# Crossbar transposes ahead of later stores, GpSimd's work in another order, and one visit split in two, in a linear-attention and MLP kernel

## The chip, the core and the metric

The kernel runs on one core of a Trainium2 chip. The metric is the device time of one execution in microseconds. The engines are called TensorE (PE in the profile; its weight loads are PEld), VectorE (DVE), ScalarE (ACT), GpSimd (POOL) and SyncE (SP). Each takes its instructions in the order in which the program wrote them; they meet through semaphores. GpSimd and SyncE also issue DMAs: GpSimd all loads (they cast from 32-bit to 16-bit floats on the way), SyncE the stores and the crossbar transposes (a DMA that turns a 16-bit tile of SBUF around).

## The reference

Four sequences (B = 4) of 768 positions, 8 heads of 64 go through an attention with exponential decay, worked out in blocks of 64 positions with a state per head; its output, as 3072 tokens of 512, goes through a two-layer MLP with an exact GELU.

```python
for b in range(nb):                      # blocks of 64 positions
    intra = np.einsum('bhic,bhjc->bhij', qb, kb) * Dmask[None]
    intra = np.einsum('bhij,bhjd->bhid', intra, vb)
    inter = np.einsum('bhid,bhde->bhie', qb * lam_pow[None], kv_state)
    out[:, :, sl] = intra + inter
    kb_dec = kb * rev_pow[None]
    kv_state = lam_block[None, :, None, None] * kv_state + np.einsum('bhsd,bhse->bhde', kb_dec, vb)
h = x @ w_in                             # 512 -> 2048
g = 0.5 * h * (1.0 + erf(h * inv_sqrt2))
return g @ w_out                         # 2048 -> 512
```

## The kernel before

**Tiling.** A chunk is 128 positions (two blocks) of one sequence; chunk n belongs to group n // 4 and sequence n % 4. There are six groups (0 to 5) of four chunks. A group of 512 tokens goes through the MLP while the attention of the next group is worked out in between: the order of the work is written out by hand (the scheduler is off).

**The MLP of a group** (`mlp`) is a list of blocks. Sixteen are `mm1`: four matmuls (512 columns, or 384 where the fourth chunk's tokens are left for later) into a bank "mh" (two of them), and a GELU on ScalarE. In group 0 the first two, in group 1 the first four have 384 columns, and a "late" block, at index 4 and 6, does the remaining 128 columns of them. Then come sixteen `mm2` blocks of four matmuls, four for each chunk's output rows; after the fourth ScalarE copies the bank to `o_sb` and SyncE stores it. `run_blocks(blocks, ahead)` runs the blocks, and before block i whatever stands in `ahead[i]`. So group 1 has blocks 0 to 32, with mm2 from 17 on, and stores after blocks 20, 24, 28 and 32.

**The attention of a chunk n.** The loads of k, q (`ask("k8 q8")`, 128 KB each) and of the V of a whole group (`V2`, four loads) are issued by GpSimd. k and q are turned into `kT`, `qT`: for chunks 0 to 7 by TensorE with copies by ScalarE (`both`), from chunk 8 on by two crossbar transposes on SyncE (`request`, lines 198 and 199). GpSimd makes `vd` (V times decay, `decay_v`, line 220) and half of `k2` (k by block, `by_block`, line 206, two copies); the other half is made by VectorE (line 211) or, for chunks 5 to 7, by ScalarE (line 209).

**A visit.** `visit(f, d)` is one run of small 64x64 matmuls on TensorE: for chunk d the scores (`sc`, from kT, qT) and the two state updates (`kv`, from k2, vd), and, between them, for chunk f, visited as d before, the outputs (`o`). Four banks "at" are taken in turn by kv, sc and o. VectorE then masks the scores (`mask`), makes t = kv + state, `mid` (its 16-bit copy; in group 1 by ScalarE), empties f's outputs into `xT` (`empty`), which the next group's MLP reads, and makes the new state from t2 = kv + t. I write a visit as (f,d), with - for none. With a merged visit there are 64 matmuls that scores and outputs share; alone there are 32.

**The order before.** In group 0's mm2 blocks (index 17 on, two chunks' blocks by turns) stand `both(4)` before block 24, then before blocks 29, 30, 31, 32 the rest of group 1: visit (-,4) before 29, (4,5) before 30, (5,6) before 31, (6,7) before 32; the V loads of group 2 stand after k2 of chunk 6. In group 1: visit (7,-) before block 1, (-,8) before 6, then (8,9), (9,10), (10,11), (11,12) before 13, 19, 25, 31. Each `request` stands at the point where its chunk's GpSimd work does (before blocks 2, 8, 14, 20), followed by the loads of the chunk after next. In group g >= 2, with n = 4(g+1), visits (n,n+1) and so on stand before blocks 7, 15, 23, 31, and a chunk's request, GpSimd work and the loads two chunks on before 0, 8, 16, 24.

So SyncE's queue holds, for instance: transposes of 12 (block 20), the four stores of group 1, transposes of 13, 14, 15, two stores of group 2, transposes of 16. SyncE takes them one by one, each when its data is there.

**Buffers.** k and q ten each, V of groups three, kT, qT and k2 four each, vd six, `o_sb` three.

Of the kernel before, what the change touches and what calls it, by code (L numbers as in the profile page):

```python
# [8 lines left out]
F32 = mybir.dt.float32  # L9
# [6 lines left out]
def kernel(  # L16
# [29 lines left out]
    work_pool = ctx.enter_context(tc.tile_pool(name="work", bufs=4))  # L46
    x_pool = ctx.enter_context(tc.tile_pool(name="x", bufs=2))
    g_pool = ctx.enter_context(tc.tile_pool(name="g", bufs=2))
    out_pool = ctx.enter_context(tc.tile_pool(name="outp", bufs=3))
    ps = ctx.enter_context(tc.tile_pool(name="ps", bufs=1, space=bass.MemoryType.PSUM))  # L50

    BANKS = dict(mh=2, mo=2, at=4)
# [4 lines left out]
    def half(i):  # L57
        return slice(i * 64, (i + 1) * 64)
# [12 lines left out]
                                         bufs=B if name == "v" else 10)  # L71
        nc.gpsimd.dma_start(t, dram[name][b, :, g * C:(g + 1) * C, :].rearrange("h si d -> si h d"))  # L72

    def load_blocks(g, name):

        t = raw["group", g, name] = qkv_pool.tile([128, 2, B * HP, D], BF16, tag=name + "g", name=name + "g_t", bufs=3)
        src = dram[name].rearrange("b (hp hi) s d -> hi s (b hp) d", hi=2)
        for u in range(2):
            for hi in range(2):
                s = g * C + u * L  # L80
                nc.gpsimd.dma_start(t[half(hi), u], src[hi, s:s + L])  # L81
# [23 lines left out]
    def ask(items):  # L105

        for item in items.split():
            name, at = item[0], item[1:]
            if name in "kqv":
                load(int(at), name)  # L110
            elif name == "V":
                load_blocks(int(at), "v")
            else:
                (load_w_in if name == "i" else load_w_out)(*(int(x) for x in at.split("-")))

    ask("k0 q0 k1 q1 v0 k2 q2 v1 k3 q3 v2 v3 i0-2 i2-5 i5-8 i8-12 i12-16 o0-4 o4-8 o8-12 o12-16 "
        "k4 q4 V1 k5 q5 k6 q6 k7 q7")

    idle = consts.tile([128, 512], BF16)
# [57 lines left out]
    def begin(n):  # L177
        c = live[n] = Chunk()
        c.n, c.g, c.b = n, n // B, n % B
        c.q, c.k = (raw.pop((n, name)) for name in "qk")  # L180
        c.v = of_group(n, "v") if c.g else raw.pop((n, "v"))
        c.kT = work_pool.tile([128, HP, C], BF16, tag="kT", name="kT")
        c.qT = work_pool.tile([128, HP, C], BF16, tag="qT", name="qT")
        return c

    def transposed(c, name, tag, eng):

        t_ps = bank([128, HP, C], BF16, tag, "t_ps")
        src, dst = (c.k, c.kT) if name == "k" else (c.q, c.qT)
        for hp in range(HP):  # L190
            nc.tensor.transpose(t_ps[:, hp, :], src[:, 2 * hp:2 * hp + 2, :], ident)
        if eng is nc.scalar:
            nc.scalar.copy(dst, t_ps)
        else:
            eng.tensor_copy(dst, t_ps)

    def dma_transposes(c):
        nc.sync.dma_start_transpose(out=c.kT, in_=c.k.rearrange("p h d -> p (h d)"))
        nc.sync.dma_start_transpose(out=c.qT, in_=c.q.rearrange("p h d -> p (h d)"))

    def by_block(c):

        c.k2 = work_pool.tile([128, 2, HP, D], BF16, tag="k2", name="k2")
        k_r = c.k.rearrange("p (hp hi) d -> p hp hi d", hi=2)
        for hi in range(2):
            (nc.vector if c.n == B else nc.gpsimd).tensor_copy(c.k2[half(hi), hi], k_r[half(hi), :, hi, :])  # L206
        for hi in range(2):
            if c.g == 1 and c.n > B:
                nc.scalar.copy(c.k2[half(hi), 1 - hi], k_r[half(1 - hi), :, hi, :])
            else:  # L210
                nc.vector.tensor_copy(c.k2[half(hi), 1 - hi], k_r[half(1 - hi), :, hi, :])  # L211

    vd = {}

    def of_group(n, name):
        return raw["group", n // B, name][:, :, n % B * HP:(n % B + 1) * HP, :]

    def decay_v(n):
        vd[n] = work_pool.tile([128, 2, HP, D], BF16, tag="vd", name="vd", bufs=6)
        nc.gpsimd.tensor_mul(vd[n], of_group(n, "v"), lam_vb)  # L220


    def scores(c):
# [12 lines left out]
        return [[(kv[half(hi), u, hp, :], c.k2[half(hi), u, hp, :], vd[c.n][half(hi), u, hp, :], True)  # L236
                 for hi in range(2)] for u in us for hp in range(HP)]

    def next_states(c, between=lambda: None):
        s0 = state[c.n]  # L240
        t1 = work_pool.tile([128, HP, D], F32, tag="t1", name="t1")
        c.mid = work_pool.tile([128, HP, D], BF16, tag="mid", name="mid")
        if c.g == NG - 1:
            nc.vector.tensor_add(c.mid, c.kv[:, 0], s0)
            return between()
        nc.vector.tensor_add(t1, c.kv[:, 0], s0)
        if c.g == 1:
            nc.scalar.copy(c.mid, t1)
        else:
            nc.vector.tensor_copy(c.mid, t1)  # L250
        between()
        t2 = work_pool.tile([128, HP, D], F32, tag="t2", name="t2")
        nc.vector.tensor_add(t2, c.kv[:, 1], t1)
        new = state[c.n + B] = work_pool.tile([128, HP, D], BF16, tag="state", name="state", bufs=7)
        nc.vector.tensor_mul(new, t2, lam_cb)  # L255

    def outputs(c):
        o = c.o = bank([128, HP, C], F32, "at", "o_ps")
# [16 lines left out]
    def empty(c):  # L275
        nc.vector.tensor_mul(xT[c.g][:, :, c.b * C:(c.b + 1) * C], c.o, lam_o)  # L276
# [6 lines left out]
                    for out_, lhsT, rhs, start in pairs[i]:  # L283
                        nc.tensor.matmul(out_, lhsT, rhs, start=start, stop=True, skip_group_check=True)  # L284

    def visit(f, d):
        f, d = (live[n] if n is not None else None for n in (f, d))
        lists = []
        if d:
            kv = states(d)  # L290
            lists.append(scores(d) + kv)
        if f:
            lists.append(outputs(f))
        issue(*lists)
        if d is None or f and f.n == 2 * B - 2:
            empty(f)
            f = None
        if d:
            mask(d)
            next_states(d, lambda: f and empty(f))  # L300


    def scores0(n):
# [36 lines left out]
    def mlp(g, n3):  # L340
# [4 lines left out]
        def mm1(kf, hi=T):  # L345
            def run():
                h_ps = bank([128, T], F32, "mh", "h_ps")
                cuts = [(0, 2 * C), (2 * C, hi)] if g == 0 and kf == 0 else [(0, hi)]
                for lo, up in cuts:
                    for ki in range(NK1):  # L350
                        nc.tensor.matmul(h_ps[:, lo:up], w_in_t[:, ki, kf * 128:(kf + 1) * 128], x_t[:, ki, lo:up],  # L351
                                         start=(ki == 0 and lo == 0), stop=(ki == NK1 - 1), skip_group_check=True)
                nc.scalar.activation(g_t[:, kf, :hi], h_ps[:, :hi], ACT.Gelu)  # L353
            return run
# [99 lines left out]
        outputs0(3)  # L454
        empty(live[3])

    def both(n):
        begin(n)
        for name in "kq":
            transposed(live[n], name, "mh", nc.scalar)  # L460

    def blocks_of(n, loads=""):
        if n > B:
            decay_v(n)
        by_block(live[n])
        ask(loads)

    def request(n):
        dma_transposes(begin(n))

    def run_blocks(blocks, ahead):
        for i, run in enumerate(blocks):
            for act in ahead.get(i, []):
                act()
            run()

    first = 1 + NK2
    run_blocks(mlp(0, n3), {
        1: [last_of_first],
        6: [make_dmask] + [lambda n=n: decay_k0(n, nc.vector) for n in range(B)],  # L480
        first: [first_states],
        first + 7: [lambda: both(4), lambda: blocks_of(4)],
        first + 12: [lambda: decay_v(4), lambda: ask("k8"), lambda: both(5), lambda: blocks_of(5, "q8"),
                     lambda: visit(None, 4)],
        first + 13: [lambda: both(6), lambda: blocks_of(6, "V2"), lambda: request(8), lambda: visit(4, 5)],
        first + 14: [lambda: both(7), lambda: blocks_of(7, "k9 q9"), lambda: visit(5, 6)],
        first + 15: [lambda: visit(6, 7)],
    })

    def prepare(n):
        decay_v(n)
        by_block(live[n])

    def load_next(n):
        if n < NG * B:
            ask(f"k{n} q{n}" + (f" V{n // B}" if n % B == 0 else ""))

    for g in range(1, NG):  # L500
        ahead = {i: [] for i in range(64)}
        if g == 1:
            ahead[1] += [lambda: visit(7, None)]
            for i, n in [(0, 8), (2, 9), (8, 10), (14, 11), (20, 12)]:
                if i:
                    ahead[i] += [lambda n=n: request(n)]
                ahead[i] += [lambda n=n: prepare(n), lambda n=n: load_next(n + 2)]
            visits = [(None, 8, 6), (8, 9, 13), (9, 10, 19), (10, 11, 25), (11, 12, 31)]
        elif g + 1 < NG:
            n = (g + 1) * B  # L510
            visits = [(n, n + 1, 7), (n + 1, n + 2, 15), (n + 2, n + 3, 23), (n + 3, n + 4, 31)]
            for i in range(B):
                m = n + i + 1
                if m < NG * B:
                    ahead[8 * i] += [lambda m=m: request(m), lambda m=m: prepare(m), lambda m=m: load_next(m + 2)]
        else:
            visits = []
        if g + 1 < NG:
            alloc_x(g + 1)
        for f, d, at in visits:  # L520
            ahead[at].insert(0, lambda f=f, d=d if d < NG * B else None: visit(f, d))
        run_blocks(mlp(g, 4 if g == 1 else 0), ahead)


# [28 lines left out]
```

## Time and profile before

| | us |
|---|---|
| runs of the kernel (three) | 223.77, 223.79, 226.64; median 223.79 |
| the profiled execution | 225.0 |
| its span, first to last instruction | 222.9 |
| busy: TensorE / weight loads | 203.4 / 99.5 |
| busy: VectorE / ScalarE / GpSimd | 76.1 / 89.7 / 107.2 |

The profile is one execution. TensorE's busy time says how long some matmul was under way; it is not a measure of its peak. A wait is named by what ended it. The DMA digits of the page stand at 9 (the engines' mean busy share, in tenths) in slices 2 to 25, that is from about 6 to 145 us, and lower afterwards. Besides the matmuls of the MLP (88.4 us in `mm1`, 83.7 in `mm2`), the largest rows are ScalarE's GELU (96 of 590 ns), GpSimd's issues of k and q (48 of about 900 ns), vd (20 of 1046 ns) and k2 (38 copies of 400 ns).

### The profile page before, as it was taken

Reading aid. Unit: us, or ns where it says so; the run is one execution under the profiler, and the core shown is the slowest. Engines: PE = TensorE matmul, PEld = TensorE weight load, DVE = VectorE, ACT = ScalarE, POOL = GpSimd, SP = SyncE. Lnnn points to the kernel's source line nnn. Section 1 sums busy time; section 2 is a strip of 40 time slices with the busy share of each in tenths; the row PEclk is TensorE's granted clock in tenths of the full one; section 3 lists DMA queues with packets and bytes.
Section 4 is the critical chain, followed back from the end, with each engine's and each line's share of the span. In section 5 each row is a group of like instructions: output and inputs, shape, how many; then the busy total and the mean of one; then the engine's idle time right before and its main releaser. Section 6 shows DMA issues by size and latency. Waiting matters only on the chain.

```text
span 222.9 us, 5215 instructions
## 1 busy us (share of the span) xinstructions
PE 203.4 (91%) x2237; PEld 99.5 (45%) x2237; DVE 76.1 (34%) x176; ACT 89.7 (40%) x161; POOL 107.2 (48%) x150
## 2 busy tenths in 40 slices
PE   7577999994999999949999599999999999999993
PEld 2334444462554444423444234444445444444452
DVE  5687004084664444314425235245303311100000
ACT  5474670393456211524512045621266412467121
POOL 8996634899399949964997344221000000000000
PEclk9999999999799999997999979999999999999999
DMA  6999999999999999999999994703243011100112
GB/s 42 145 156 194 205 206 178 174 170 102 183 99 122 138 214 117 136 145 127 71 101 184 121 140 96 50 17 104 75 131 59 3 50 69 72 3 0 47 49 94
DMA packets 100887, 24.46 MB, mean 110 GB/s; under 512 B 93056, under 2 KB 97920, under 8 KB 100864
## 3 DMA queue, kind: packets, MB, share of 16 engines
q0 software_dynamic: 79712, 13.64, 84.3%
q1 hardware_dynamic: 21152, 10.50, 20.4%
q8 instruction: 17, 0.28, 0.5%
q14 instruction: 6, 0.05, 0.1%
HBM read 27.27 MB, written 6.29 MB: 151 GB/s over the span
## 4 chain that ended last, share of the span: by engine, by line
PE 65%; DMA 18%; POOL 11%; DVE 2%; issue 1%; ACT 0%; POOLq 0%
PE h_ps L351 31%; PE o_ps L380 27%; DMA qT<-q_t 6%; DMA w_out_t<-in_moe_w_out_dram 5%; DMA vg_t<-in_v_dram 5%; DMA w_in_t<-in_moe_w_in_dram 3%; PE sc_ps L284 2%; POOL k_t L72 2%; POOL q_t L72 2%; POOL vd L220 2%; PE o_ps L284 2%; PE o_ps L391 2%; POOL v_t L72 2%; POOL vg_t L81 1%; PE kv_ps L284 1%; POOL k L206 1%
## 5 line engine op out<-in xcount | busy, mean ns | idle before, releaser
L351 PE MATMUL h_ps<-x_t,w_in_t 128*128 128x512 bf16 (+3 forms) x388 | 88.4, 385 | 2.7 <-DMA w_in_t<-in_moe_w_in_dram 1.5
L380 PE MATMUL o_ps<-w_out_t,g_t 128*128 128x512 bf16 x368 | 83.7, 382 | 0.0
L353 ACT ACTIVATE g_t<-h_ps 128x512 bf16<-128x512 f32 (+1 forms) x96 | 56.7, 590 | 41.6 <-PE h_ps L351 41.6
L351 PEld LDWEIGHTS <-w_in_t 128*128 128x128 bf16 x388 | 37.8, 100 | 48.8 <-issue 8.1
L380 PEld LDWEIGHTS <-g_t 128*128 128x128 bf16 x368 | 34.8, 98 | 40.8 <-issue 0.5
L372 ACT COPY o_sb<-o_ps 128x512 f32<-128x512 f32 (+1 forms) x25 | 14.2, 569 | 73.2 <-PE o_ps L380 63.4
L231 DVE TENSOR_TENSOR sm<-sc_ps,dmask 128x512 bf16<-128x512 f32 x20 | 13.8, 691 | 81.3 <-PE sc_ps L284 81.2
L220 POOL TENSOR_TENSOR vd<-vg_t,lam_v 128x512 bf16<-128x512 bf16 x20 | 20.9, 1046 | 14.0 <-DMA vg_t<-in_v_dram 13.0
L206 POOL COPY k<-k_t 64x256 bf16<-64x256 bf16 x38 | 15.2, 400 | 20.0 <-PE o_ps L284 18.9
L72 POOL DMA_DIRECT2D k_t<-in_k_dram x24 | 22.1, 920 | 2.2 <-DMA w_out_t<-in_moe_w_out_dram 1.7
L72 POOL DMA_DIRECT2D q_t<-in_q_dram x24 | 21.5, 896 | 2.5 <-DMA w_out_t<-in_moe_w_out_dram 1.7
L276 DVE TENSOR_TENSOR x_t<-o_ps,lam_o 128x512 bf16<-128x512 f32 x24 | 16.4, 682 | 11.2 <-PE o_ps L284 11.2
L81 POOL DMA_DIRECT2D vg_t<-in_v_dram x20 | 16.4, 833 | 4.3 <-DMA w_out_t<-in_moe_w_out_dram 3.3
L284 PE MATMUL sc_ps<-qT,kT 64*64 64x64 bf16 (+1 forms) x352 | 10.4, 197 | 5.9 <-DMA qT<-q_t 5.4
L284 PEld LDWEIGHTS <-kT 64*64 64x64 bf16 (+1 forms) x352 | 7.8, 107 | 14.0 <-issue 10.2
L284 PE MATMUL kv_ps<-vd,k 64*64 64x64 bf16 x288 | 8.1, 193 | 2.9 <-POOL k L206 2.7
L211 DVE COPY k<-k_t 64x256 bf16<-64x256 bf16 x34 | 8.7, 257 | 2.2 <-ACT g_t L353 1.6
L284 PE MATMUL o_ps<-sm,vg_t 64*64 64x64 bf16 x320 | 8.8, 195 | 0.0
L284 PEld LDWEIGHTS <-k 64*64 64x64 bf16 x288 | 6.3, 108 | 3.1 <-POOL k L206 3.1
L414 PE MATMUL idle_ps<-idle 128*128 128x512 bf16 x17 | 6.4, 492 | 1.2 <-DVE idle L120 1.2
L255 DVE TENSOR_TENSOR state<-t,lam_c 128x256 bf16<-128x256 f32 x16 | 7.2, 451 | 0.5
L284 PEld LDWEIGHTS <-vg_t 64*64 64x64 bf16 x320 | 7.0, 110 | 0.0
(62 smaller groups left out, 117.4 us busy)
## 6 DMA issues: line engine op xcount, KB each, us to landing
out_dram<-o_sb SPq DMA_DIRECT2D x23, 256.0 KB, 2.6
k_t<-in_k_dram POOLq DMA_DIRECT2D x24, 128.0 KB, 4.8
q_t<-in_q_dram POOLq DMA_DIRECT2D x24, 128.0 KB, 5.1
vg_t<-in_v_dram POOLq DMA_DIRECT2D x20, 128.0 KB, 7.0
w_out_t<-in_moe_w_out_dram POOLq DMA_DIRECT2D x4, 512.0 KB, 12.5
w_in_t<-in_moe_w_in_dram POOLq DMA_DIRECT2D x4, 256.0 KB, 8.5
w_in_t<-in_moe_w_in_dram POOLq DMA_DIRECT2D x4, 192.0 KB, 6.3
v_t<-in_v_dram POOLq DMA_DIRECT2D x4, 128.0 KB, 4.6
```

The source lines that it names most:

```text
L72: nc.gpsimd.dma_start(t, dram[name][b, :, g * C:(g + 1) * C, :].rearrange("h si d -> si h d"))
L81: nc.gpsimd.dma_start(t[half(hi), u], src[hi, s:s + L])
L206: (nc.vector if c.n == B else nc.gpsimd).tensor_copy(c.k2[half(hi), hi], k_r[half(hi), :, hi, :])
L211: nc.vector.tensor_copy(c.k2[half(hi), 1 - hi], k_r[half(1 - hi), :, hi, :])
L220: nc.gpsimd.tensor_mul(vd[n], of_group(n, "v"), lam_vb)
L231: nc.vector.tensor_mul(c.sm, c.sc, dmask)
L276: nc.vector.tensor_mul(xT[c.g][:, :, c.b * C:(c.b + 1) * C], c.o, lam_o)
L284: nc.tensor.matmul(out_, lhsT, rhs, start=start, stop=True, skip_group_check=True)
L351: nc.tensor.matmul(h_ps[:, lo:up], w_in_t[:, ki, kf * 128:(kf + 1) * 128], x_t[:, ki, lo:up], start=(ki == 0 and lo == 0), stop=(ki == NK1 ...
L353: nc.scalar.activation(g_t[:, kf, :hi], h_ps[:, :hi], ACT.Gelu)
L372: nc.scalar.copy(o_sb, ps_)
L380: nc.tensor.matmul(om[io], g_t[:, kf, io * C:(io + 1) * C], w_out_t[:, kf, :], start=(kf == 0), stop=(kf == NK2 - 1))
```

## The change

- **First loads.** v3 is loaded after the first piece of W_in (`i0-2`); the next piece `i2-5` is split into `i2-3` and `i3-5`.
- **Group 1's chunks, in group 0.** `both(4)` stands before block 25. `begin` (which takes the kT and qT buffers) of 4 to 7 is called at the start. vd and k2 of chunks 5, 6 and 7 stand after the visit before them, so that on ScalarE `mid` precedes the k2 copies; the V loads of group 2 (with k9, q9) stand after vd and k2 of chunk 7.
- **Last visit of group 0 in two.** Visit (6,7) before block 32 becomes visit (6,-) and visit (-,7) after block 32. The second half of chunk 6's state (t2 and state) is held (`hold`) until after visit (6,-).
- **Group 1's plan.** Visits (7,-) before block 2, (-,8) before 8, the others as before. Loads are asked for by pairs of chunks (`fetch`), transposes by pairs (`request`): 9 in block 0, 10 and 11 in block 3, 12 and 13 in block 9, 14 and 15 in block 21. k2's GpSimd half (`values`) and its VectorE half (`keys`) are placed apart.
- **Groups 2 to 4.** Loads of n+4, n+5 in block 2 and n+6, n+7 in block 18; transposes of n+4, n+5 in block 8 and n+6, n+7 in block 18, where n = 4(g+1).
- **Buffers.** kT, qT, k2: six instead of four; `o_sb`: six instead of three. Group 1's first `mm1` block, too, is cut at column 256.

SyncE's queue is then: T8, two stores, T9, T10, T11, T12, T13, one store of group 1, T14, T15, three stores, T16 to T19, four stores of group 2, and so on (T8: both transposes of chunk 8). GpSimd's from chunk 7 on: vd and k2 of 7, V of group 2, k9, q9, vd and k2 of 8, loads of 10 and 11, vd and k2 of 9, loads of 12 and 13, vd and k2 of 10, V of group 3, vd and k2 of 11, vd and k2 of 12, loads of 14 and 15, vd and k2 of 13, loads of 16 and 17, V of group 4.

```diff
-    out_pool = ctx.enter_context(tc.tile_pool(name="outp", bufs=3))
+    out_pool = ctx.enter_context(tc.tile_pool(name="outp", bufs=6))
...
-    ask("k0 q0 k1 q1 v0 k2 q2 v1 k3 q3 v2 v3 i0-2 i2-5 i5-8 i8-12 i12-16 o0-4 o4-8 o8-12 o12-16 "
+    ask("k0 q0 k1 q1 v0 k2 q2 v1 k3 q3 v2 i0-2 v3 i2-3 i3-5 i5-8 i8-12 i12-16 o0-4 o4-8 o8-12 o12-16 "
         "k4 q4 V1 k5 q5 k6 q6 k7 q7")
...
-        c.kT = work_pool.tile([128, HP, C], BF16, tag="kT", name="kT")
-        c.qT = work_pool.tile([128, HP, C], BF16, tag="qT", name="qT")
+        c.kT = work_pool.tile([128, HP, C], BF16, tag="kT", name="kT", bufs=6)
+        c.qT = work_pool.tile([128, HP, C], BF16, tag="qT", name="qT", bufs=6)
...
-    def next_states(c, between=lambda: None):
+    def next_states(c, between, hold):
...
-        t2 = work_pool.tile([128, HP, D], F32, tag="t2", name="t2")
-        nc.vector.tensor_add(t2, c.kv[:, 1], t1)
-        new = state[c.n + B] = work_pool.tile([128, HP, D], BF16, tag="state", name="state", bufs=7)
-        nc.vector.tensor_mul(new, t2, lam_cb)
+        def rest():
+            t2 = work_pool.tile([128, HP, D], F32, tag="t2", name="t2")
+            nc.vector.tensor_add(t2, c.kv[:, 1], t1)
+            new = state[c.n + B] = work_pool.tile([128, HP, D], BF16, tag="state", name="state", bufs=7)
+            nc.vector.tensor_mul(new, t2, lam_cb)
+
+        if hold:
+            c.rest = rest
+        else:
+            rest()
...
-        if d is None or f and f.n == 2 * B - 2:
+        if d is None:
             empty(f)
...
-                cuts = [(0, 2 * C), (2 * C, hi)] if g == 0 and kf == 0 else [(0, hi)]
+                cuts = [(0, 2 * C), (2 * C, hi)] if g < 2 and kf == 0 else [(0, hi)]
...
-        first + 7: [lambda: both(4), lambda: blocks_of(4)],
-        first + 12: [lambda: decay_v(4), lambda: ask("k8"), lambda: both(5), lambda: blocks_of(5, "q8"),
-                     lambda: visit(None, 4)],
-        first + 13: [lambda: both(6), lambda: blocks_of(6, "V2"), lambda: request(8), lambda: visit(4, 5)],
-        first + 14: [lambda: both(7), lambda: blocks_of(7, "k9 q9"), lambda: visit(5, 6)],
-        first + 15: [lambda: visit(6, 7)],
-    })
+        first + 8: [lambda: both(4), lambda: by_block(live[4], nc.vector, nc.vector)],
+        first + 12: [lambda: decay_v(4), lambda: ask("k8"), lambda: both(5), lambda: visit(None, 4),
+                     lambda: decay_v(5), lambda: by_block(live[5], nc.gpsimd, nc.scalar), lambda: ask("q8")],
+        first + 13: [lambda: both(6), lambda: visit(4, 5), lambda: decay_v(6),
+                     lambda: by_block(live[6], nc.gpsimd, nc.scalar)],
+        first + 14: [lambda: both(7), lambda: visit(5, 6, hold=True), lambda: decay_v(7),
+                     lambda: by_block(live[7], nc.gpsimd, nc.scalar), lambda: ask("V2 k9 q9"), lambda: begin(8),
+                     lambda: request(8)],
+    })
+    visit(6, None)
+    live[6].rest()
+    visit(None, 7)
...
+    def values(n):
+        decay_v(n)
+        by_block(live[n], nc.gpsimd, None)
+
+    def keys(n):
+        by_block(live[n], None, nc.vector)
+
+    def fetch(*ns):
+        ns = [n for n in ns if n < NG * B]
+        for n in ns:
+            ask(f"k{n} q{n}")
+        if ns and ns[0] % B == 0 and ns[0] > 2 * B:
+            ask(f"V{ns[0] // B}")
+        for n in ns:
+            begin(n)
...
+                0: [lambda: values(n), lambda: request(n + 1)],
+                1: [lambda: fetch(n + 2, n + 3)],
+                2: [lambda: visit(n - 1, None)],
+                3: [lambda: keys(n), lambda: request(n + 2, n + 3)],
+                4: [lambda: values(n + 1)],
+                5: [lambda: ask(f"k{n + 4} q{n + 4} k{n + 5} q{n + 5}")],
+                8: [lambda: visit(None, n)],
+                9: [lambda: values(n + 2), lambda: ask("V3"), lambda: begin(n + 4), lambda: begin(n + 5),
+                    lambda: request(n + 4, n + 5)],
+                10: [lambda: keys(n + 1)],
+                13: [lambda: visit(n, n + 1)],
+                14: [lambda: values(n + 3)],
+                15: [lambda: keys(n + 2)],
+                19: [lambda: visit(n + 1, n + 2)],
+                20: [lambda: values(n + 4)],
+                21: [lambda: keys(n + 3), lambda: fetch(n + 6, n + 7),
+                     lambda: request(n + 6, n + 7)],
+                25: [lambda: visit(n + 2, n + 3)],
+                27: [lambda: keys(n + 4)],
+                31: [lambda: visit(n + 3, n + 4)],
...
+            0: [lambda: values(n + 1)],
+            2: [lambda: keys(n + 1), lambda: fetch(n + 4, n + 5)],
+            7: [lambda: visit(n, n + 1)],
+            8: [lambda: values(n + 2), lambda: more and request(n + 4, n + 5)],
+            10: [lambda: keys(n + 2)],
+            15: [lambda: visit(n + 1, n + 2)],
+            16: [lambda: values(n + 3)],
+            18: [lambda: keys(n + 3), lambda: fetch(n + 6, n + 7), lambda: more and request(n + 6, n + 7)],
+            23: [lambda: visit(n + 2, n + 3)],
+            24: [lambda: more and values(n + 4)],
+            26: [lambda: more and keys(n + 4)],
+            31: [lambda: visit(n + 3, n + 4 if more else None)],
```

## The prediction, made before the changed kernel ran

> **What bounds it now.** I read the slices of the page, then the waits of TensorE, then its timeline around each wait, the clock there, and last the queues that ended the waits. TensorE is busy for 91% of the span; the page's granted clock dips three times:
>
> ```profile
> PEclk9999999999799999997999979999999999999999
> ```
>
> TensorE's waits (total us, times, longest), then its timeline (start, us, instruction, idle time before it):
>
> ```profile
> PE sc_ps L284 <- DMA qT<-q_t: 5.4, 2, 3.0
> PE kv_ps L284 <- POOL k L206: 2.7, 1, 2.7
> ```
> ```profile
> 54.16 0.22 PE L284 MATMUL kv_ps<-vd,k 64*64 64x64 bf16 x2 [2.74 <-POOL k L206]
> 99.19 0.22 PE L284 MATMUL sc_ps<-qT,kT 64*64 64x64 bf16 x2 [3.03 <-DMA qT<-q_t]
> 126.34 0.22 PE L284 MATMUL sc_ps<-qT,kT 64*64 64x64 bf16 x2 [2.36 <-DMA qT<-q_t]
> ```
>
> So three waits, at the visits (6,7), (12,13) and (15,16). After each, the stretches view (length, busy times, granted clock, DMA) has half clock:
>
> ```profile
> 55.63:59.04 3.41, 3.41 (x41) 1.80 (x39) 2.98 (x8) 1.28 (x3) 0.69 (x1) 0.50 1.66 171
> 100.00:103.42 3.42, 3.42 (x9) 1.22 (x8) 2.79 (x8) 0.64 (x2) 0.33 (x1) 0.50 2.26 161
> 127.31:130.72 3.41, 3.21 (x9) 1.01 (x8) 2.63 (x8) 0.58 (x1) 3.29 (x5) 0.50 0.57 44
> ```
>
> Half of 3.41 is 1.7 lost: 32 matmuls of the chain took 8.70 after the second wait, 7.01 elsewhere. A wait of 3 thus costs about 4.7.
>
> What ended them. GpSimd issues the four V loads of group 2 before it makes vd and k2 of chunk 7, and later waits for those loads:
>
> ```profile
> 49.36 3.30 POOL L81 DMA_DIRECT2D vg_t<-in_v_dram  x4
> 52.73 1.04 POOL L220 TENSOR_TENSOR vd<-vg_t,lam_v 128x512 bf16<-128x512 bf16 x1
> 53.72 0.84 POOL L206 COPY k<-k_t 64x256 bf16<-64x256 bf16 x2
> ...
> 60.01 1.04 POOL L220 TENSOR_TENSOR vd<-vg_t,lam_v 128x512 bf16<-128x512 bf16 x1 [3.69 <-DMA vg_t<-in_v_dram]
> 61.00 0.84 POOL L206 COPY k<-k_t 64x256 bf16<-64x256 bf16 x2
> 61.79 0.92 POOL L72 DMA_DIRECT2D k_t<-in_k_dram  x1
> 62.70 0.89 POOL L72 DMA_DIRECT2D q_t<-in_q_dram  x1
> ```
>
> On SyncE the transposes of chunk 13, and of 16, stand behind stores that wait for TensorE:
>
> ```profile
> 78.50 12.24 SPq L373 DMA_DIRECT2D out_dram<-o_sb  x4
> 90.83 1.23 SPq L198 DMA_TRANSPOSE kT<-k_t  x1
> 92.16 1.31 SPq L199 DMA_TRANSPOSE qT<-q_t  x1
> ...
> 114.40 4.56 SPq L373 DMA_DIRECT2D out_dram<-o_sb  x2
> 119.05 1.26 SPq L198 DMA_TRANSPOSE kT<-k_t  x1
> 120.41 1.21 SPq L199 DMA_TRANSPOSE qT<-q_t  x1
> ```
>
> q of chunk 13 had landed at 82.6, so its place in the queue cost some 9 us. q of chunk 16 landed at 118.6: there the load was late too.
>
> **The change, part by part.**
>
> *Start.* v3 now follows the first W_in piece, which TensorE awaited for 1.08 at 17.47; one v issue is 0.87, so the first layer starts up to 0.87 earlier. The gain dies: the transposes of chunks 5, 6, 7 need q, landed at 44.0, 46.5 and 48.9, and TensorE took up q of chunk 7 at 48.96. Two more W_in issues (0.6 each) lie in GpSimd's waits at 18.6 to 21.7 (0.37, 0.67, 0.96). Taken: 0 (-0.5 to +0.3).
>
> *ScalarE in group 1.* mid now precedes the k2 copies: the loop mask 0.6, t 0.4, mid 0.4, k2 0.82 adds at most 0.4 a visit, inside the same waits for q. Visit (5,6) ends near 49.95, as before.
>
> *Last visit in two, vd and k2 of 7 before V of group 2.* k2 of chunk 7 is ready near 51.3, not 54.56. TensorE: two mm2 blocks (0.88 each) to 51.7; visit (6,-) 0.62 to 52.3. The kv bank of chunk 7 is chunk 6's, which the held t2 still reads: empty 0.65 and t2 0.41 on VectorE come first, so visit (-,7) ends near 53.8. Two 384-column blocks of 0.66 to 55.1; visit (7,-) waits for state, mask, t, mid: 55.8, and the gelu behind mid frees the bank near 56.0. Blocks 2, 3 (0.66, plus gelu pace) to 57.4; 4, 5, 7 at 0.87 and the late block at 0.97: visit (-,8) starts at 61.0, kv at 61.3. Price of the split: 0.6 for a second run of 32 small matmuls (64 in a merged visit take only 0.67) and two small waits of 0.6.
>
> But chunk 8's vd needs V of group 2, now issued at 51.3 to 54.6 instead of 49.4 to 52.7. Its last quarter landed at 59.84, in a queue also filled by the transposes of chunk 8 (6.4 to 6.8 to land there; 2.3 when alone at 133 to 140). One transpose is now done sooner; I keep 59.84. Then k2 of 8 is ready at 61.85, as in the rows above. Four load issues (3.62, before: two), vd 1.04 and copies 0.84 put k2 of 9 at 67.4; visit (8,9) ends at 67.75 against 70.02: gain 2.2. If V lands later by all of its 1.95, gain 0.25; if TensorE alone paced it (61.65 + 5 x 0.87 + 0.67 = 66.7), gain 3.3.
>
> *Group 1 from there.* TensorE needs 5.95 from visit to visit (69.35, 75.31, 81.26, 87.21). GpSimd needs 5.55 for four loads, vd, copies: hidden by 0.4. Chunk 10: k issued 61.9, landed +4.0, transposes at 66 and 67.3, qT +5.1 (its row before) = 72.4, due 73.05: hidden by 0.6. V of group 3: issued 73.0 to 76.3, last +7.2 (its row) = 82.7 (73.4 to 80.65 before), vd and k2 of 12 ready 84.6, due 85.2: hidden by 0.6. If such cover goes, see the first rival.
>
> *Chunk 13 (block 9 of group 1, ahead of all stores).* k lands near 75, transposes issue by 77.6 and land by 85; due 93.9. The wait of 3.03 and its 1.7 go: 4.74. Next late is only x_t (0.24 at 89.95, kept).
>
> *Chunk 16.* Its loads go out near 90 instead of 112, its transposes after the stores of group 1, landed near 105; due 117. Gone: 2.36; of the half clock 0.92 (28 matmuls 7.12 against 6.20); 0.4 by a shorter VectorE chain (x_t 2.05 after the visit's start at 158.99, 2.45 here): 3.7.
>
> *SyncE.* The transposes of 14 and 15 wait for loads issued at 83 to 86.5, landed near 90.5; behind them stand stores two to four of group 1, ready at 79 to 88, now leaving near 94. ScalarE would be waiting for o_sb (3.64 before 118.01 with three buffers); six cover these four. GpSimd's wait for buffers (18.9 in all) was off the path: 0. VectorE gets k2's other half as before: 0.
>
> **Clock rule.** After waits of 2.36 to 3.03 this trace shows half clock for 3.41. The Trainium skill, "TensorE: Matmul & The Clock Gate", Part 1 (The HAM clock gate), says the clock halves after an idle window of about 3.4 us. By that rule no wait here would have halved it, and the sum would lose its clock terms (1.7 and 0.92 of the two later gains) and be 8.0. The rows differ, and the sum goes by them.
>
> **Sum.** 2.2 + 4.74 + 3.7 = 10.6; span 222.9 - 10.6 = 212.3. The profiled execution took 225.0, 2.1 more than its span: 214.4. The runs' median is 223.79, 1.2 below that execution; most of what can differ between them is waits that go, so I take 214.2. With the bounds of the early part (+2.0, -1.1): 213 to 216.5.
>
> **Rivals.**
> 1. *A new wait in group 1* (0.20): chunk 10's transposes or group 3's V miss their 0.6. For it: transposes in a loaded queue take 7.0 to 7.8 (at 90 to 100). Then qT lands at 74.9, a wait of 1.9 and 1.7 of clock: 218. Against: the same neighbours before gave 5.1.
> 2. *Slower: GpSimd's issues wait* (0.05). Between 25 and 38 an issue waited until the DMA eight issues earlier had landed, 1.25 to 2.6 from issue to issue. If the twelve loads that now precede k2 of 9, 10, 11 are paced like that, each costs 1.6 more than 0.91: 19 us and three clock losses of 1.7, 236 in all. It decides from 0.9 per issue. Against: landings of 3.4 to 8 us are mostly under eight issues (7.3), and no issue waited from 50 on.
> 3. *Nothing gained* (0.05): the waits move to other transposes, since they meet as many loads there: 222.6. Against: the transposes of 13 and 16 were late by their queue place and by a load that now goes out 20 us sooner; price: 214.2 + 4.74 + 3.7.
> 4. *Better* (0.04): V lands early, 211.8 to 213.
>
> Forecast 0.66. The range 211.8 to 218.6 reaches through most of rival 1. Faster by over 2% (below 219.3, about what a measurement can tell) 0.89, within 0.06, slower 0.05.
>
> **What would show it.** No wait on qT above 0.5 and no half clock after 60; k2 of 7 done before the V issues; visit (8,9) ending near 67.8, its wait put down to GpSimd's copies; transposes of 12 and 13 before the first group-1 store. Wrong if a matmul of a visit waits over 1.5 for qT, or GpSimd's load issues have idle time before them.

## The result and the profile after

The changed kernel took 214.87 us (median of four, 214.72 to 215.47); the kernel before 225.21 (four, 223.77 to 227.52). The ratio is 0.957 with an interval of 0.948 to 0.966: faster. The profiled execution took 215.47, of which 213.7 is its span (before: 225.0 and 222.9). Single runs of the kernel before lie between 223.6 and 227.5 in all groups of runs; the profiled one is an ordinary one among them.

The clock row of the changed kernel's page, to set against the row with three dips:

```profile
PEclk9969999999999999999999999999999999999998
```

The dips in the middle are gone; what is left are the start-up and the end. The waits of TensorE (us in total, times, longest) after the change, three of its lines:

```profile
PE t_ps L191 <- DMA q_t<-in_q_dram: 3.4, 4, 1.8
PE h_ps L359 <- DVE x_t L284: 1.6, 2, 1.2
...
PE o_ps L292 <- DMA v_t<-in_v_dram: 1.1, 1, 1.1
```

The line `sc_ps <- DMA qT` with its 5.4, and `kv_ps <- POOL k` with its 2.7, are no longer there. The wait for x_t has grown: its longest is 1.2, and was 0.5. TensorE's timeline has it behind the visit (15,16), and it shows the largest of the waits for q as well (start, us, instruction, idle time before it):

```profile
46.34 0.40 PE L191 MATMUL t_ps<-ident,q_t 128*128 128x128 bf16 x4 [1.84 <-DMA q_t<-in_q_dram]
...
120.52 6.20 PE L359 MATMUL h_ps<-x_t,w_in_t 128*128 128x512 bf16 x28 [1.15 <-DVE x_t L284]
```

SyncE's queue after the change, group 1's part of it:

```profile
72.89 1.19 SPq L198 DMA_TRANSPOSE kT<-k_t  x1
74.87 1.20 SPq L199 DMA_TRANSPOSE qT<-q_t  x1
76.17 1.21 SPq L198 DMA_TRANSPOSE kT<-k_t  x1
77.48 1.21 SPq L199 DMA_TRANSPOSE qT<-q_t  x1
78.78 0.55 SPq L381 DMA_DIRECT2D out_dram<-o_sb  x1
...
94.79 1.60 SPq L381 DMA_DIRECT2D out_dram<-o_sb  x3
96.48 2.51 SPq L198 DMA_TRANSPOSE kT<-k_t  x1
99.09 1.96 SPq L199 DMA_TRANSPOSE qT<-q_t  x1
```

The pairs of the chunks 12 and 13 are issued by 78.7, before the first store of group 1; before, chunk 13's went out at 90.8 and 92.2 behind four stores. The pair of 96.5 and 99.1 is chunk 16's; before, it went out at 119.1 and 120.4. GpSimd's queue around its moved work:

```profile
50.23 1.04 POOL L221 TENSOR_TENSOR vd<-vg_t,lam_v 128x512 bf16<-128x512 bf16 x1
51.22 0.94 POOL L208 COPY k<-k_t 64x256 bf16<-64x256 bf16 x2
52.10 3.31 POOL L81 DMA_DIRECT2D vg_t<-in_v_dram  x4
...
60.84 1.04 POOL L221 TENSOR_TENSOR vd<-vg_t,lam_v 128x512 bf16<-128x512 bf16 x1 [3.65 <-DMA vg_t<-in_v_dram]
```

vd and k2 of chunk 7 are now done, at 52.16, ahead of the V loads, which came first before; and the wait for V, 3.69 then, is still 3.65.

Where the time went can be read from the starts of the visits, which delimit stretches with the same work:

| stretch between visits | before | after | saved | the change's part |
|---|---|---|---|---|
| start to (8,9) | 69.28 | 67.99 | 1.29 | GpSimd's order, first loads, split, and what else stands there |
| (8,9) to (11,12) | 17.86 | 17.85 | 0.01 | |
| (11,12) to (12,13) | 12.05 | 8.63 | 3.42 | wait for qT of 13 |
| (12,13) to (13,14) | 9.36 | 7.76 | 1.60 | its half clock |
| (13,14) to (14,15) | 7.68 | 7.75 | -0.07 | |
| (14,15) to (15,16) | 10.11 | 7.68 | 2.43 | wait for qT of 16 |
| (15,16) to (16,17) | 9.54 | 8.99 | 0.55 | its half clock, less a wait for x_t |
| (16,17) to the end | 87.0 | 87.0 | 0 | |

The sum is 9.2 of span. By this table the places of two pairs of transposes, those of chunks 13 and 16, carry 7.9 of it.

### The profile page after: what moved, and what is told of

It is laid out like the page before. It is cut to its first block, busy times and chain, and to the rows that moved or that the text cites. A ratio compares the mean times of both kernels' runs of the same rounds, so it can differ in the third digit from the quotient of the medians.

```text
span 213.7 us, 5227 instructions
## 1 busy us (share of the span) xinstructions
PE 200.6 (94%) x2241; PEld 99.7 (47%) x2241; DVE 80.2 (38%) x176; ACT 90.0 (42%) x161; POOL 108.9 (51%) x152
## 4 chain that ended last, share of the span: by engine, by line
PE 72%; DMA 11%; POOL 10%; DVE 3%; issue 1%; ACT 1%; POOLq 0%
PE h_ps L359 32%; PE o_ps L388 32%; DMA w_out_t<-in_moe_w_out_dram 7%; DMA q_t<-in_q_dram 4%; POOL w_in_t L100 3%; PE sc_ps L292 3%; PE o_ps L292 2%; POOL k_t L72 2%; POOL q_t L72 2%; POOL v_t L72 2%; PE o_ps L399 2%; PE kv_ps L292 1%; POOL w_out_t L103 1%; DVE x_t L284 1%; DVE sm L232 1%
## 5 line engine op out<-in xcount | busy, mean ns | idle before, releaser
L359 PE MATMUL h_ps<-x_t,w_in_t 128*128 128x512 bf16 (+3 forms) x392 | 84.9, 372 | 2.1 <-DVE x_t L284 1.6
L388 PE MATMUL o_ps<-w_out_t,g_t 128*128 128x512 bf16 x368 | 82.8, 379 | 0.0
L359 PEld LDWEIGHTS <-w_in_t 128*128 128x128 bf16 x392 | 37.1, 98 | 44.3 <-issue 3.7
L208 POOL COPY k<-k_t 64x256 bf16<-64x256 bf16 x38 | 15.7, 412 | 1.1
L212 DVE COPY k<-k_t 64x256 bf16<-64x256 bf16 x34 | 12.1, 356 | 0.5
L258 DVE TENSOR_TENSOR state<-t,lam_c 128x256 bf16<-128x256 f32 x16 | 8.2, 511 | 0.5
L100 POOL DMA_DIRECT2D w_in_t<-in_moe_w_in_dram x12 | 7.6, 676 | 0.4 <-DMA v_t<-in_v_dram 0.2
```

Of the source, the lines that this page charges most:

```text
L100: nc.gpsimd.dma_start(w_in_t[half(1 - hi), :, f], w_in_r[hi, :, :, f])
L208: same.tensor_copy(c.k2[half(hi), hi], k_r[half(hi), :, hi, :])
L388: nc.tensor.matmul(om[io], g_t[:, kf, io * C:(io + 1) * C], w_out_t[:, kf, :], start=(kf == 0), stop=(kf == NK2 - 1))
```

## Experiments

Three theories were tested. The theory of the prediction: the place of two pairs of transposes in SyncE's queue gives most, GpSimd's order gives some. A rival to it: the late waits would reappear at other transposes. And for the half clock: its cost is apart from the wait itself and can be taken away apart. The eleven runs came in three groups, each on one chip beside the kernel before: its median was 225.15 for y1, y2, x1, x2; 224.38 for y3, y4, x3, z1; 224.54 for z2, z3 and the second measurement of the changed kernel.

### One transpose pair moved, nothing else

To the kernel before, in group 1:

```diff
+            ahead[20] += [lambda: request(13)]
...
-  [lambda m=m: request(m), ...
+  [lambda m=m: m == 13 or request(m), ...
```

> The kernel before, with one part of the change alone: the two transposes of chunk 13 are asked for right behind those of chunk 12, ahead of the four stores of group 1. Theory (the place in SyncE's queue made them late): q of chunk 13 lands near 82.6, its transposes issue by 84 and land by 90; visit (12,13) no longer waits for qT, the half clock near 100 goes, the span falls by 4.7 (3.03 + 1.7) to about 218; the waits at visits (6,7) and (15,16) stay. Rival (the loaded transfers make them late): the wait at (12,13) stays above 2 us, or one as long appears at (13,14), and the span stays within 1 of 222.9.

220.89 (220.52 to 221.59), ratio 0.982 (0.978 to 0.987). SyncE's queue in this kernel:

```profile
81.21 1.73 SPq L198 DMA_TRANSPOSE kT<-k_t  x1
83.04 1.22 SPq L199 DMA_TRANSPOSE qT<-q_t  x1
84.36 7.77 SPq L373 DMA_DIRECT2D out_dram<-o_sb  x4
```

The pair now stands ahead of the four stores. From visit (11,12) to (12,13) it is 8.65, what the changed kernel needs there (8.63), and nothing waits for qT at (12,13). From (12,13) to (13,14) it is 7.68 at the full clock, where the kernel before took 9.36. The wait at (15,16) stays, with 2.12; 0.54 is new at (16,17). So one pair's place alone brings 4 us (every run is below every run of the kernel before beside it), and at the next visits no wait as long takes its place.

### Both pairs moved, nothing else

To the edit above, for group 2:

```diff
+            if g == 2:
+                ahead[18] += [lambda: request(16)]
...
+  m in (13, 16) or request(m)
```

> The kernel before, with two things moved on SyncE alone: the transposes of chunk 13 ahead of the four stores of group 1, and those of chunk 16 ahead of the stores of group 2. The loads are as before. Theory (both later waits come of the place in SyncE's queue; k and q of chunk 16 are loaded before 98 already): both waits for qT at (12,13) and (15,16) fall below 0.5, the span falls by 8.4 to about 214.5, up to 216 if the transposes of chunk 17, still behind two stores, make visit (16,17) wait; the wait at (6,7) stays. Rival (my prediction's reading: chunk 16's load was late too): the wait at (15,16) stays at about 2, span near 218.2.

217.08 (216.53 to 219.45), ratio 0.969 (0.964 to 0.975). SyncE's queue, and below it TensorE's waits:

```profile
97.80 1.65 SPq L198 DMA_TRANSPOSE kT<-k_t  x1
99.55 1.29 SPq L199 DMA_TRANSPOSE qT<-q_t  x1
109.94 12.23 SPq L373 DMA_DIRECT2D out_dram<-o_sb  x4
```
```profile
PE kv_ps L284 <- POOL k L206: 2.2, 1, 2.2
...
PE h_ps L351 <- DVE x_t L276: 1.3, 2, 0.8
```

Chunk 16's pair is out at 97.8 and 99.6, ahead of four stores that wait for TensorE; no visit waits for qT any more. Its loads are where the kernel before has them. That corrects one reading of the prediction. GpSimd's queue in the kernel before:

```profile
89.95 0.92 POOL L72 DMA_DIRECT2D k_t<-in_k_dram  x1
90.87 0.89 POOL L72 DMA_DIRECT2D q_t<-in_q_dram  x1
91.75 3.27 POOL L81 DMA_DIRECT2D vg_t<-in_v_dram  x4
```

These two loads, just ahead of V of group 4, are chunk 16's; q landed at 97.6. The row near 112, with a q that landed at 118.6, was chunk 20's. Nothing was late about the load of chunk 16: the pair merely stood behind stores until 119. This experiment gains 7.3 us with two requests moved; the changed kernel, measured beside its own neighbours on another chip, gains 9.6 (224.54 to 214.97).

### GpSimd's order alone

To the kernel before: V of group 2, and chunk 8's request, a visit later.

```diff
-  lambda: blocks_of(6, "V2"), lambda: request(8), ...
+  lambda: blocks_of(6), ...
-  lambda: blocks_of(7, "k9 q9"), ...
+  lambda: blocks_of(7, "V2 k9 q9"), lambda: request(8), ...
```

> The kernel before, with GpSimd's order alone changed: the four V loads of group 2 stand after vd and k2 of chunk 7; visits stay where they were. Theory (in the early part the landing of that V sets the pace, so that the swap by itself only moves the wait): visit (6,7) waits under 0.5, the V lands 0.8 to 1.2 later than before, near 60.8, and visit (-,8), now due near 58.3, waits 3 to 4.5 for k2 of chunk 8, with a half clock or without; span within 1.5 of 222.9. Rival (the swap itself is the gain): no wait above 1.5 at (-,8), visit (8,9) ends 3 to 4 sooner than 70.0, span near 219.

224.94 against 224.38, with four runs far apart: 226.54, 225.42, 224.47 and 219.57. The first three show no gain. The last is 4.5 below every run of the kernel before on that chip, and its span of 217.6 is near the 219 that the rival named. Its mean granted clock was 0.997, that of the others 0.974 to 0.984; as 3.41 us at half clock cost 0.0077 of the mean over such a span, it can't have had the three half clocks of the traced run. It was not traced, so whether GpSimd's order alone gains something stays open. GpSimd's queue and TensorE's timeline in the run of 226.54:

```profile
51.31 3.31 POOL L81 DMA_DIRECT2D vg_t<-in_v_dram  x4
60.30 1.04 POOL L220 TENSOR_TENSOR vd<-vg_t,lam_v 128x512 bf16<-128x512 bf16 x1 [3.90 <-DMA vg_t<-in_v_dram]
```
```profile
61.73 0.77 PE L284 MATMUL kv_ps<-vd,k 64*64 64x64 bf16 x16 [2.19 <-POOL k L206]
```

In that run the wait of 2.74 for k2 at (6,7) is down to 0.49, for another engine; 2.19 appears two visits later, at (-,8), again for k2, because V of group 2 is still awaited. A half clock from 63.0 to 66.4 follows it, and (8,9) starts at 70.28, a microsecond later than before. V's last part landed at 60.1 here, at 59.8 before and at 60.7 after the change, with issues that start between 49.4 and 52.1; in the twelve traces that show it, it is between 59.5 and 61.1. What holds it there was not tried.

### The changed kernel with the first loads in their old order

```diff
-    ask("... v2 i0-2 v3 i2-3 i3-5 i5-8 ...
+    ask("... v2 v3 i0-2 i2-5 i5-8 ...
```

> The changed kernel with the first loads in the order of before (v3 ahead of the first W_in piece, i2-5 in one). Theory (the two more W_in issues push all later loads back, which I had put at 0): the last W_out piece lands near 37.2 and q of chunk 5 near 44, not 38.2 and 46.3; visit (5,6) ends near 50, not 52.2; visit (8,9) ends 1 earlier, near 67.7; span 1 shorter, about 212.2, though the first layer starts up to 0.9 later. Rival (the later landings were that execution's own): W_out and q of chunk 5 land as in the changed kernel within 0.3, the span stays within 0.4 of 213.1.

215.23 (214.71 to 215.86), ratio 0.957. The theory was right on the landings and wrong on the time. TensorE's timeline in this kernel:

```profile
47.38 0.40 PE L191 MATMUL t_ps<-ident,q_t 128*128 128x128 bf16 x4 [0.81 <-DMA q_t<-in_q_dram]
...
62.65 0.77 PE L292 MATMUL kv_ps<-vd,k 64*64 64x64 bf16 x16 [0.47 <-POOL k L208]
```

q of chunk 5 landed at 44.1 instead of 46.3, and the visit (5,6) ended 1.2 earlier; then TensorE met the same V of group 2 (61.05) at (-,8), waited for chunk 8's k2, and (8,9) ended at 68.93, much as in the changed kernel (68.72). Over all traces the old order has q of chunk 5 at 43.9 to 44.8 (eight traces), the new one at 44.9 to 46.9 (five). The new order costs the load about a microsecond, and V of group 2 hides it. The last W_out piece does not tell the orders apart (37.0 to 38.5 in the old one, 37.5 to 38.5 in the new). In every trace q of chunk 5 is issued 0.3 after that piece has landed; what differs is the way from there to its landing, 5.8 to 7.3 in the old order and 7.1 to 8.1 in the new.

### The changed kernel with one visit (6,7)

```diff
-    visit(6, None)
-    live[6].rest()
-    visit(None, 7)
+        first + 15: [lambda: visit(6, 7)],
```

with hold gone from visit (5,6), and the old condition for chunk 6's early empty.

> The changed kernel with visit (6,7) in one again, before block 32, and nothing held back; GpSimd still makes vd and k2 of chunk 7 ahead of V of group 2. Theory (GpSimd's order ends the wait, the split only costs a second run of small matmuls and the chain of VectorE behind it): no wait above 1 for k2 at visit (6,7), TensorE reaches visit (8,9) 0.5 to 1 earlier, span 0.5 to 1 shorter. Rival (the split is what covers ScalarE's k2 copy of chunk 7, done at 54.1 in the changed kernel): visit (6,7) starts near 53.3 and waits for that copy and then for VectorE, span 0.5 to 2 longer.

214.98 (214.66 to 215.68), ratio 0.956. Neither side was right: there is a small wait (TensorE's timeline),

```profile
53.35 0.21 PE L292 MATMUL kv_ps<-vd,k 64*64 64x64 bf16 x1 [0.49 <-ACT k L212]
```

and the time is that of the changed kernel. The split is worth nothing that these runs can see.

### The changed kernel with three output buffers

```diff
-    out_pool = ctx.enter_context(tc.tile_pool(name="outp", bufs=6))
+    out_pool = ctx.enter_context(tc.tile_pool(name="outp", bufs=3))
```

> The changed kernel with three buffers for o_sb instead of six. The prediction had ScalarE waiting for o_sb then, because transposes stand before the stores in SyncE's queue. Theory: ScalarE waits 1 to 3 for a store at the end of group 2, where four stores leave together near 115.5; GELUs behind it come late and TensorE waits up to 1; span 0 to 1 longer than 213.1. Rival (three are enough): no wait of ScalarE for a store above 0.5, span within 0.4.

216.26 (215.03 to 217.73), ratio 0.964 (0.959 to 0.969), 1.3 above the changed kernel's 214.97 by the medians; the intervals of the two ratios just overlap. ScalarE's timeline, TensorE's, and SyncE's queue:

```profile
123.39 0.59 ACT L380 COPY o_sb<-o_ps 128x512 f32<-128x512 f32 x1 [7.41 <-DMA out_dram<-o_sb]
```
```profile
124.52 2.75 PE L359 MATMUL h_ps<-x_t,w_in_t 128*128 128x512 bf16 x12 [2.17 <-ACT g_t L361]
```
```profile
115.70 1.25 SPq L199 DMA_TRANSPOSE qT<-q_t  x1
117.04 7.29 SPq L381 DMA_DIRECT2D out_dram<-o_sb  x4
```

The first store of group 2 had its data at 108.3, went out at 117.04 behind the last of the transposes, and landed at 123.3. With three buffers ScalarE's fourth copy stands 7.4 us for that landing, the GELU is behind it, and TensorE waits 2.17 for g_t. Transposes ahead of stores need somewhere to keep the outputs: at the end of group 2, not in group 1 as the prediction had it.

### What a wait of 3 costs in clock

To the kernel before, matmuls on idle data ahead of the wait at (12,13):

```diff
+        if g == 2:
+            ahead[7].insert(0, lambda: keep_warm(10))
```

> The kernel before, with ten more 128x512 matmuls on zeros (they belong to no output) ahead of visit (12,13), that is inside its wait of 3.03 for qT. Theory (the clock term is apart from the wait, and comes of TensorE's idleness): the wait for qT shrinks to about 0.8 after 2.2 of idle matmuls, the visit starts where it did (near 99.2), no half clock follows at 100, and the span falls by 1.7 to about 221. Rival (half clock has another cause, or costs nothing): the clock still falls to 0.5 after the visit, the span stays at 222.9 within 0.5.

223.41 (220.4 to 224.0), ratio 0.989 (0.980 to 0.997). TensorE's timeline, and the stretch after the visit (us from and to, length, busy time and instructions of PE, PEld, VectorE, ScalarE and GpSimd, granted clock, DMA share, GB/s) in this kernel, then the same stretch in the kernel before:

```profile
94.98 2.32 PE L414 MATMUL idle_ps<-idle 128*128 128x512 bf16 x10
99.32 0.22 PE L284 MATMUL sc_ps<-qT,kT 64*64 64x64 bf16 x2 [2.02 <-DMA qT<-q_t]
```
```profile
99.32:107.00 7.68, 7.62 (x96) 3.68 (x97) 3.12 (x8) 4.18 (x7) 3.85 (x6) 1.00 1.35 111
```
```profile
99.19:108.55 9.36, 9.36 (x97) 4.10 (x97) 3.12 (x8) 4.18 (x7) 5.28 (x9) 0.82 1.70 116
```

The visit starts when it did, since qT has not come sooner, and the stretch behind it is 1.68 shorter, at the full clock. That is the 1.7 of the prediction, measured by itself: the price of one half clock. Of the whole kernel's time the runs say less: the median is 1.7 below that of the kernel before, but the ranges meet (220.4 to 224.0 and 223.6 to 226.2), and the trace differs elsewhere too: no half clock after the wait at (6,7), and one at 125.8. That it was the idle matmuls which kept the clock up is taken up in the last section.

### A faster version: x_t ahead of the mask

The waits for x_t were the only ones above 0.4 that the changed kernel's trace has from group 2 on. One condition makes VectorE write x_t of a group's last chunk before the next chunk's mask:

```diff
-        if d is None:
+        if d is None or f and f.b == B - 1:
```

> The changed kernel, where VectorE empties the outputs of a group's last chunk ahead of the mask, t and mid of the visit before the next group's MLP. Theory (TensorE's waits of 1.15 and 0.49 for x_t stand behind those three steps): x_t is ready 0.8 after the visit's start plus its 0.7, under the 0.88 of the mm2 block; both waits go, nothing else comes late; span 1.5 shorter, near 211.5. Rival (the next visit waits for the later mask, or the wait is TensorE's own): span within 0.5.

214.36 (213.28 to 214.62), ratio 0.954 (0.950 to 0.957). The waits for x_t are gone, and from the end of (8,9) to the end of the span it is 142.7, against 145.0; but q of chunk 5 landed at 46.9 and a half clock from 48.4 to 51.8 followed, so that (8,9) ended at 70.1, 1.4 late, and the span fell by 0.8, not 1.5. With the old order of the first loads besides:

> The changed kernel with the first loads in the order of before and with VectorE's emptying of a group's last chunk put first. Theory: q of chunk 5 lands near 44.3; TensorE's waits for x_t stay away; but visit (-,8) is held by V of group 2 (landing at 60 to 61 in every trace so far), so that the early part gains at most 0.5; span 211 to 211.8, that is 1.5 to 2 less than the changed kernel's on this chip. Rival (the early part is TensorE's own): visit (8,9) ends before 67.5, span below 210.8.

213.10 (six runs, 212.62 to 214.22), ratio 0.947 (0.943 to 0.952). TensorE's longest waits:

```profile
PE t_ps L191 <- DMA q_t<-in_q_dram: 2.8, 4, 1.0
PE h_ps L359 <- DMA w_in_t<-in_moe_w_in_dram: 1.4, 1, 1.4
```

Every one of its six runs is below every one of the changed kernel's six on the same chip (214.65 to 216.01): this version is faster than both kernels, by 1.9 than the changed one in the median. The merged visit besides:

> As the one before, with visit (6,7) in one again. Theory (held by V of group 2, the split is worth nothing): the same time within 0.4. Rival (the split costs its second run of small matmuls, 0.6, or saves the wait for ScalarE's copy): 0.6 or more apart.

213.72 (212.71 to 214.76). That is 0.6 above the version without it, at the border that the expectation drew between theory and rival, with ranges that overlap for the most part: the merged visit brings nothing more, and whether it costs something these runs do not settle.

### The changed kernel once more

> The changed kernel itself, for its landings and its time beside the next two on the same chip. Theory (the first loads' order makes the later landings): the last W_out piece lands at 37.6 or later and q of chunk 5 at 45 or later, as in the four traces with that order so far (37.7 to 38.5, 45.2 to 46.9); span 212.9 to 213.7. Rival (chance): q of chunk 5 lands near 44.3, as in the six traces with the order of before.

214.97 (214.65 to 216.01), ratio 0.956 (0.951 to 0.960). Its waits, of TensorE:

```profile
PE h_ps L359 <- DVE x_t L284: 1.7, 3, 0.8
...
PE sc_ps L292 <- DMA qT<-q_t: 1.2, 2, 0.8
```

Here qT is awaited, 0.82 at (9,10): this is the first rival's thin cover of 0.6, used up in this execution and not in the other. The longest wait for x_t is 0.79, not 1.15. The expectation's bounds were missed by a little: the last W_out piece landed at 37.52 and q of chunk 5 at 44.94, just below 37.6 and 45, and the span is 214.2.

## Why the prediction was right, and where its steps were not

The forecast of 214.2 missed the median by 0.7, and of the signs it named all but one held in the first trace: no wait for qT over 0.5, no half clock after 60, chunk 7's k2 before the V issues, the pairs of 12 and 13 before group 1's stores. The sign that failed is visit (8,9). Term by term:

- **Chunk 13, 4.74 predicted:** 3.42 and 1.60, together 5.0. Shown by moving that pair alone (3.40 and 1.68 at the same places), and its clock part by the idle matmuls (1.68). Right in mechanism and size.
- **Chunk 16, 3.7 predicted:** 3.0 (2.43 and 0.55) in the first trace, 3.3 (2.43 and 0.91) in the second. The mechanism is the queue alone; that "Chunk 16's loads go out near 90 instead of 112" was a row put to the wrong chunk, and moving the pair with the loads left alone disproves it. It did not harm the number, because the pair was due at the same place either way. What made it smaller is the term "0.4 by a shorter VectorE chain". The 2.05 of that term was read at visit (19,20), where chunk 20 is of the last group and VectorE makes mid in one instruction; at (15,16) it takes two, t and a cast, and x_t is ready 2.44 after the visit's start in the second trace, much as in the kernel before (2.43). In the first trace it is even 2.81. VectorE's timeline there, and GpSimd's:

```profile
118.16 0.69 DVE L232 TENSOR_TENSOR sm<-sc_ps,dmask 128x512 bf16<-128x512 f32 x1 [4.28 <-PE sc_ps L292]
118.76 0.41 DVE L247 TENSOR_TENSOR t<-kv_ps,state 128x256 f32<-128x256 f32 x1
119.21 0.66 DVE L251 CAST mid<-t 128x256 bf16<-128x256 f32 x1
119.79 0.68 DVE L284 TENSOR_TENSOR x_t<-o_ps,lam_o 128x512 bf16<-128x512 f32 x1
```
```profile
118.68 1.04 POOL L221 TENSOR_TENSOR vd<-vg_t,lam_v 128x512 bf16<-128x512 bf16 x1
```

  The cast to mid takes 0.66 and ends 0.15 after vd; with no GpSimd vd or copy beside it, in the kernel with x_t first, the same cast takes 0.29, and so it does in the changed kernel's second trace, where it does not fall into a vd. The Trainium skill, "SBUF — State Buffer" ("SBUF: two separate sides"), says that VectorE in a two-port mode and GpSimd lock each other out of a shared port pair for a whole instruction; these two rows agree with it.
- **The early part, 2.2 predicted:** 1.3; (8,9) ended at 68.72, not 67.75. The mis-sized term is V of group 2, "I keep 59.84": it landed at 60.68, 0.84 later, in the profiled execution, and the stated bound (later by up to 1.95) covers that. Chunk 9's k2 was then done at 68.2 instead of 67.4. TensorE came to (8,9) by its own work at the same time: (-,8) had started 1.95 later than the 61.0 that it was given. So no wait for GpSimd's copies shows there, as the prediction expected, though they were ready only as TensorE took them up.
- **The start, 0 predicted:** q of chunk 5 is about a microsecond later, not equal; with the old order put back nothing is gained, because V of group 2 is later still. The 0 was right for another reason than the one given. And it was not sure: in the kernel with x_t first, with the same first loads, q landed at 46.9, a half clock followed, and (8,9) ended 1.7 later than with the old order besides.
- **The split, two waits of 0.6:** the first did not come. kv of 7 starts at 54.64, before the t2 of chunk 6 that the prediction had it wait for (55.30), so it does not take the bank that this t2 reads. The second, for mid at (7,-), was 0.33. Taking the split out of the changed kernel changes nothing.
- **Six output buffers, "six cover these four":** six did; with three, the wait was not at the four stores of group 1 but at the end of group 2, with 7.4 of ScalarE and 2.2 of TensorE, some 1.3 of the time.
- **The rivals:** waits that move (the third) are seen only in the trace with GpSimd's order changed alone. A new wait in group 1 (the first) came in one of two traces, at 0.8 and with no half clock. The second, issues of GpSimd that wait, did not come after 50; its price of 236 was too low by its own terms, which add up to about 238.

The clock terms were kept against the rule of the page, and the two stretches that lost their half clock, each 1.68 shorter, show that this was right.

The rest of the change (GpSimd's order, the first loads, the split, the other pairs and buffers): the changed kernel is 2.1 faster than the kernel with the two pairs alone (217.08 to 214.97, on two chips). What carries this stays open. GpSimd's order alone made three runs of four no faster and one 4.5 faster; in its trace the later waits for qT grew to 4.2 and 3.1. The order of the first loads and the split, removed from the changed kernel one by one, cost nothing.

## What to carry to other kernels

An in-order queue that holds both stores, which wait for compute, and loads or transposes, which compute waits for, delays the second kind by as long as the first is not ready: look for a store with a long span (12.2 here) just ahead of a transfer whose data had long landed. Move the transfer, not the wait, and give the outputs enough buffers to stay in until the store comes. And a wait of 2 to 3 us of TensorE may cost another 1.7 in clock, depending on where it falls, so count the stretch behind it too.

## What the runs showed that was not expected

Half clock came in steps of 3.41 us, on a grid that does not follow the wait: 55.63, 100.00 and 127.31 of the kernel before are 13 and 8 steps of 3.413 apart. Whether a wait is followed by it is not decided by its length. It was after waits of 2.74, 3.03 and 2.36 (before), 2.19, 4.22 and 3.08 (GpSimd's order alone), 2.24 (both pairs), 1.97 (x_t first), and twice, for 6.8 us, after 2.56 (one pair). It was not after 2.12 at (15,16) in that kernel, nor after 2.17 with three output buffers, nor after 2.23 at 54.7 in the kernel with idle matmuls, nor after its 2.02. In that same kernel it was, at 125.8, around waits of 1.92 and 0.65.

What these waits do to single steps of the grid tells them apart. The stretches view gives from and to, length, TensorE's busy time and instructions, granted clock, DMA share and GB/s. First three steps of the kernel before, each up to the start of a half clock; then two of the kernel with one pair moved, around its wait of 2.12; then two of the kernel with idle matmuls:

```profile
52.22:55.63 3.41, 1.36 (x36) 1.00 2.04 136
96.59:100.00 3.41, 0.81 (x65) 1.00 2.04 155
123.90:127.31 3.41, 1.05 (x67) 1.00 0.94 144
```
```profile
118.78:122.20 3.42, 1.52 (x8) 1.00 2.37 175
122.20:125.61 3.41, 2.24 (x71) 1.00 1.27 97
```
```profile
95.05:98.47 3.42, 2.25 (x11) 1.00 2.19 147
98.47:101.88 3.41, 2.50 (x72) 1.00 1.74 157
```

TensorE was idle for 2.05, 2.60 and 2.36 of the first three steps, and half clock began where each ended. The wait of 2.12 fell across a border, so that its two steps were idle for 1.90 and 1.17, and none followed. In all thirteen traces, from 20 to 200 us, nine steps at full clock had TensorE idle for 2.05 or more, and each was followed by half clock; no step idle for 1.77 or less was, if those already at half clock are left aside. Of the three between, one of 1.90 was and the others, 1.90 and 1.98, were not. In the start-up this does not hold (half clock followed steps idle for 1.35, 1.46 and 1.66), and why it lasted two steps once is not shown.

It also answers for the idle matmuls: they fill 2.25 of the step from 95.05, which would else have been idle nearly throughout, so the clock was kept by them and not only by where the grid lay.

The Trainium skill, "TensorE: Matmul & The Clock Gate" (Part 1, The HAM clock gate), puts the half clock after an idle window of about 3.4 us and calls the window free-running. The grid agrees with the second. The nine steps do not agree with the first: only one of them was idle throughout (97.13 to 100.55 with GpSimd's order alone), and by it the three dips of the kernel before would not be there.
